# Attention block: the last block's normalisation on VectorE in another order (spread, product, spread, product by column halves)

## The chip, the cores and the metric

One core of a Trainium2 chip. The metric is the device time of one execution in microseconds (us), the median of several runs. The profile's span (first to last instruction) is some 1.8 us shorter than the device time of the same execution: 410.1 against 411.93 for the profiled run of the kernel before. Ends and differences below are taken from the traces' nanoseconds: sums of the rounded figures that the lines show can be off by 0.01 us, also in the prediction.

## The reference, cut to what matters

```python
B, S, D, H = 1, 2048, 448, 16          # bf16; head width 28
qkv = x @ wqkv
scores = jnp.einsum("bhqd,bhkd->bhqk", q, k) * (Dh ** -0.5)
p = softmax(scores)
o = jnp.einsum("bhqk,bhkd->bhqd", p, v)
return o.transpose(...).reshape(B, S, D) @ wo
```

The kernel leaves the softmax's division to the end: it sums exp(scores) along with the products with v, and divides o by that sum before the projection with wo.

## The kernel before: the parts that count

A schedule of some 400 us computes four groups of four heads for four blocks of 512 queries. ScalarE computes 425 exponentials of 128x1024. What follows is the end, for the last group and the last 512 queries. `PO` holds, in PSUM, four heads of 32 rows each, and row 28 of each 32 is the sum. The transpose by 32x32 blocks (128x512, 0.72 us) brings the sums into columns, the reciprocal is taken of 16 columns (0.25 us), and a second transpose, of a broadcast, spreads each reciprocal over the 32 rows of its head (0.45 and 0.40 us for its two halves).

```python
    def norm_dve(src, dt, dr, den):
        nc.vector.transpose(out=dt, in_=src)                      # DT, 512 columns
        nc.vector.reciprocal(out=dr, in_=dt[:, Dh::HP])           # DR, 16 columns
        n = QW // HP // 2
        for hf in range(2):                                       # "spread" 0 and 1
            nc.vector.transpose(out=den(hf), in_=dr[:, hf * n:(hf + 1) * n]
                ...to_broadcast([P, n, HP]))
    # ... (cut: the schedule)
    norm_dve(PO[:], DT[:], DR[:], lambda hf: DEN[hf][:])
    for hf in range(2):                                           # "product" 0 and 1
        nc.vector.tensor_tensor(out=OTL[hf][:], in0=PO[:, hf * hw:(hf + 1) * hw], in1=DEN[hf][:], op=ALU.mult)
        for tq in (2 * hf, 2 * hf + 1):                           # blocks 0,1 and 2,3 of 128 queries
            nc.tensor.matmul(out=fb[tq], lhsT=OTL[hf][:, (tq % 2) * P:(tq % 2 + 1) * P], rhs=WO[:, g, :], ...)
    for tq in range(TPC):
        if tq in SPLIT[c]:                                        # block 2
            nc.vector.tensor_tensor(out=OUTF[tq][:], in0=fb[tq], in1=part(c, tq), op=ALU.add)
        else:                                                     # blocks 0, 1, 3
            nc.scalar.copy(out=OUTF[tq][:], in_=fb[tq])
        (nc.scalar if tq == TPC - 1 else nc.sync).dma_start(out=out_last[:, tq, :], in_=OUTF[tq][:])
```

## Time and profile before

| | kernel before |
|---|---|
| device time, median of 3 runs | 412.26 us (411.98 to 412.35) |
| span of the profiled run | 410.1 us |
| ScalarE's exponentials | 390.8 us in 425 instructions, back to back |
| first exponential starts | 11.20 us |
| transpose of the sums (DT) starts | 402.90 us |
| last store's issue ends | 407.33 us |

The time splits into three stretches: up to the first exponential, the long row of exponentials, and the tail from DT on. The prediction shows the tail's lines with neighbours of one form merged. Narrow slices of the timeline give VectorE's four instructions one by one (start, length, both in us):

```profile
403.94 0.45 DVE L824 STREAM_TRANSPOSE DEN<-DR 128x256 f32<-128x256 f32 x1
404.31 0.40 DVE L824 STREAM_TRANSPOSE DEN<-DR 128x256 f32<-128x256 f32 x1
404.63 0.38 DVE L1243 TENSOR_TENSOR OTL<-PO,DEN 128x256 bf16<-128x256 f32 x1
404.94 0.41 DVE L1243 TENSOR_TENSOR OTL<-PO,DEN 128x256 bf16<-128x256 f32 x1
```

Each of the last three starts 0.07 to 0.08 us before its forerunner ends. None of the three needs what its direct forerunner wrote: product 0 needs spread 0, which lies two back.

### The profile page before, as it was taken

How to read it: one execution, taken by the hardware profiler on the slowest of the kernel's cores; microseconds unless marked ns; L12 is line 12 of the kernel's file. 1: busy time of each engine (PE TensorE's matmuls, PEld its weight loads, DVE VectorE, ACT ScalarE, POOL GpSimd, SP SyncE). 2: the span in 40 equal slices, each digit the busy share in tenths (PEclk: the TensorE clock that was granted, in tenths of full speed). 3: DMA queues.
4: the chain of work that ended last, by engine and by line, in shares of the span. 5: the costliest groups of instructions: out<-in, count | busy, mean ns of one | idle time of the engine just before them, and what ended most of it. 6: DMA issues, size and time to landing. Idle time of an engine off the chain costs nothing.

```text
span 410.1 us, 7564 instructions
## 1 busy us (share of the span) xinstructions
PE 362.4 (88%) x2613; PEld 120.9 (29%) x2613; DVE 395.4 (96%) x701; ACT 397.6 (97%) x437; POOL 225.6 (55%) x217
## 2 busy tenths in 40 slices
PE   8998989898998989899897988989898898989795
PEld 5333232222232232323222232232222222222222
DVE  6999999999999999999999999999999999999995
ACT  4999999999999999999999999999999999999993
POOL 3046557464656656465555646556464655747560
PEclk9999999999999999999999999999999999999999
DMA  9441021012301002111300000000410000001012
GB/s 206 67 74 30 2 57 32 15 53 49 78 2 39 8 28 30 20 38 29 81 18 26 22 15 24 12 26 21 88 38 7 30 12 26 22 27 47 2 71 90
DMA packets 36213, 16.03 MB, mean 39 GB/s; under 512 B 28816, under 2 KB 33296, under 8 KB 36176
## 3 DMA queue, kind: packets, MB, share of 16 engines
q1 hardware_dynamic: 35568, 15.35, 16.2%
q8 instruction: 20, 0.33, 0.3%
q10 hardware_dynamic: 608, 0.22, 0.2%
q14 instruction: 17, 0.14, 0.1%
HBM read 6.91 MB, written 1.96 MB: 22 GB/s over the span
## 4 chain that ended last, share of the span: by engine, by line
ACT 83%; PE 8%; issue 7%; DVE 1%; ACTq 0%
ACT PTA L1121 83%; PE PA L808 3%; PE PO L977 1%; PE PA L355 1%; PE PO L677 0%; ACT RRB L860 0%; PE PD L476 0%; PE PD L376 0%; PE PD L606 0%; PE PD L808 0%; ACT OUTF L1250 0%; PE PO L606 0%; PE PO L476 0%; PE PD L758 0%; DVE DEN L824 0%
## 5 line engine op out<-in xcount | busy, mean ns | idle before, releaser
L1121 ACT ACTIVATE PTA<-PA 128x1024 bf16<-128x1024 f32 x425 | 390.8, 1245 | 0.1
L925 POOL TENSOR_TENSOR DG<-DV,DU 128x512 f16<-128x512 f16 x174 | 200.7, 1155 | 166.1 <-DVE DV L922 156.8
L808 PE MATMUL PA<-QB,KB 64*128 64x512 bf16 x850 | 167.0, 379 | 40.3 <-ACT PTA L1121 38.1
L808 PEld LDWEIGHTS <-KB 64*128 64x128 bf16 x1024 | 66.9, 92 | 185.8 <-issue 177.4
L919 DVE TENSOR_SCALAR DU<-PD 128x512 f16<-128x512 uint16 x174 | 117.4, 679 | 2.7 <-PE PD L808 2.3
L922 DVE SCALAR_TENSOR_TENSOR DV<-PD,DU 128x512 f16<-128x512 uint16 x174 | 117.9, 681 | 1.3
L938 DVE SCALAR_TENSOR_TENSOR PTD<-PD,DG 128x512 uint16<-128x512 f32 x174 | 117.8, 677 | 0.2 <-POOL DG L925 0.2
L977 PE MATMUL PO<-PTA,VA 128*32 128x512 bf16 x850 | 84.9, 386 | 0.0
L808 PE MATMUL PD<-QB,KB 64*128 64x512 bf16 x174 | 64.7, 376 | 1.1 <-DVE PTD L938 0.6
L977 PE MATMUL PO<-PTD,VA 128*32 128x512 bf16 x174 | 60.0, 386 | 0.0
L977 PEld LDWEIGHTS <-VA 128*32 128x32 bf16 x1024 | 18.8, 94 | 45.8 <-issue 45.3
L900 POOL TENSOR_TENSOR OT<-OSB,RRB 128x512 bf16<-128x512 f32 x15 | 19.1, 1270 | 5.4 <-DVE PTD L938 1.9
L606 PE MATMUL PO<-XT,WQP 112*128 112x512 bf16 x56 | 18.5, 386 | 0.0
L476 PE MATMUL PO<-XT,WKP 112*128 112x512 bf16 x52 | 16.4, 385 | 0.1
L677 PEld LDWEIGHTS <-XT 112*128 112x128 bf16 x256 | 13.4, 98 | 10.4 <-issue 10.2
L677 PE MATMUL PO<-WV,XT 112*128 112x112 bf16 x208 | 16.0, 214 | 0.0
L1082 PE MATMUL PO<-zrow,zeros 128*128 128x512 bf16 x45 | 15.4, 386 | 0.0
L616 DVE TENSOR_SCALAR QB<-PO,offscol 128x512 bf16<-128x512 f32 x14 | 10.4, 743 | 1.0 <-PE PO L606 0.8
L511 DVE TENSOR_SCALAR KB<-PO,onescol 128x512 bf16<-128x512 f32 x12 | 8.9, 740 | 0.0
L885 DVE COPY OSB<-PO 128x512 f32<-128x512 f32 x13 | 8.9, 683 | 0.0
L758 PE MATMUL PO<-WO,OT 128*128 128x448 bf16 x28 | 8.2, 358 | 0.0
L515 DVE TENSOR_REDUCE KPART<-KB 128x1 f32<-128x512 bf16 x12 | 7.9, 661 | 0.0
(97 smaller groups left out, 120.6 us busy)
## 6 DMA issues: line engine op xcount, KB each, us to landing
RRB<-SCR SPq DMA_DIRECT2D x15, 256.0 KB
QB<-QP SPq DMA_DIRECT2D x56, 32.0 KB
KB<-NK SPq DMA_DIRECT2D x12, 128.0 KB
XS<-in_x_dram SPq DMA_DIRECT2D x3, 448.0 KB
out_dram<-XS SPq DMA_DIRECT2D x3, 448.0 KB
QB<-QB SPq DMA_DIRECT2D x28, 32.0 KB
KB<-KB SPq DMA_DIRECT2D x6, 128.0 KB
WV<-in_wqkv_dram SPq DMA_DIRECT2D x1, 392.0 KB
```

The costliest lines, as they stand in the source:

```text
L476: ops = chain_mm(CC, lambda cc: nc.tensor.matmul(out=ap(), lhsT=WKP[g][:, cc, :], rhs=XT[sc][cc // 2][0:CK, cc % 2, :], start=(cc == 0), s ...
L606: ops = chain_mm(CC, lambda cc: nc.tensor.matmul(out=ap(), lhsT=WQP[g][:, cc, :], rhs=XT[c][cc // 2][0:CK, cc % 2, :], start=(cc == 0), st ...
L677: nc.tensor.matmul(out=ap()[:, jj * GW:(jj + 1) * GW], lhsT=XT[jq][cc // 2][0:CK, cc % 2, jj * P:(jj + 1) * P], rhs=WV[:, cc, g * GW:(g + ...
L808: nc.tensor.matmul(out=ap, lhsT=KB[g % 2][i // 2][a:a + 64, j * P:(j + 1) * P], rhs=QB[w % NQB][i // 2][a:a + 64, :], start=True, stop=Tru ...
L900: o5 = add(Op("POOL", 1.22, lambda: nc.gpsimd.tensor_tensor(out=OT[g][c][:], in0=OSB[b][:], in1=RRB[b][:], op=ALU.mult), deps=o4, prio=-10 ...
L919: p1 = add(Op("DVE", P1, lambda: nc.vector.tensor_scalar(out=DU[b][:], in0=lo, scalar1=SIG / 65536, scalar2=SIG * (SS - 0.5), op0=ALU.mult ...
L922: p2 = add(Op("DVE", P1, lambda: nc.vector.scalar_tensor_tensor(out=DV[b][:], in0=lo, scalar=65536 * (SS - 0.5 + CE / C3), in1=DU[b][:], o ...
L925: gq = add(Op("POOL", PTT, lambda: nc.gpsimd.tensor_tensor(out=DG[b][:], in0=DV[b][:], in1=DU[b][:], op=ALU.mult), deps=[p2], prio=n, kind ...
L938: f = add(Op("DVE", P1, lambda: nc.vector.scalar_tensor_tensor(out=PTD[st["s"].idx][:].bitcast(U16), in0=PX[slot.idx][:], scalar=EBITS + C ...
L977: nc.tensor.matmul(out=PO[HP * st:HP * (st + 1), :], lhsT=VA[g][:, j, st, :], rhs=r["p"][i][1](), start=first, stop=last, tile_position=(0 ...
L1082: nc.tensor.matmul(out=PO[:], lhsT=zeros[:], rhs=zrow[:], start=first, stop=first, skip_group_check=True)
L1121: nc.scalar.activation(out=PTA[pslot.idx][:, 0:len(ns) * QW], in_=PA[s.idx][:, 0:len(ns) * QW], func=ACT.Exp, bias=ACT_BIAS, scale=ACT_SCALE)
```

## The change

The intent: TensorE's first projection needs product 0, product 0 needs spread 0 alone, so take spread 1 out of its way.

```diff
-    def norm_dve(src, dt, dr, den):
+    def norm_dve(src, dt, dr, den, then):
 ...
         for hf in range(2):
             nc.vector.transpose(out=den(hf), ...)
+            then(hf)
 ...
-    norm_dve(PO[:], DT[:], DR[:], lambda hf: DEN[hf][:])
-    for hf in range(2):
+
+    def half_out(hf):
         nc.vector.tensor_tensor(out=OTL[hf][:], ...)
         for tq in (2 * hf, 2 * hf + 1):
             nc.tensor.matmul(out=fb[tq], ...)
+    norm_dve(PO[:], DT[:], DR[:], lambda hf: DEN[hf][:], half_out)
```

No instruction is added or removed, and TensorE's order stays.

## The prediction

> **What bounds the kernel now.** I read the page's busy row first, then the chain that ended last as a whole, then that chain for the last ten microseconds, then the timeline and the short windows of the tail. The page says who is busy, and by whom the end is set:
>
> ```profile
> PE 362.4 (88%) x2613; PEld 120.9 (29%) x2613; DVE 395.4 (96%) x701; ACT 397.6 (97%) x437; POOL 225.6 (55%) x217
> ACT 83%; PE 8%; issue 7%; DVE 1%; ACTq 0%
> ```
>
> ScalarE (ACT) is busy 97% of the 410.1 us span and carries 83% of the chain: its 425 exponentials (390.8 us) set the pace. VectorE (DVE) is at 96%, but carries only 1% of the chain. The change touches neither loop. It reorders four VectorE instructions that run once, after the last exponential (which ends at 402.32 us). So the steady state stays, and the question is how much of the tail depends on these four. The chain in the tail (start, length, what):
>
> ```profile
> 402.90 0.73 DVE DT L820
> 403.63 0.02 issue
> 403.65 0.27 DVE DR L821
> 403.92 0.02 issue
> 403.94 0.77 DVE DEN L824 x2
> 404.71 0.32 DVE OTL L1243
> 405.03 0.05 issue
> 405.08 0.38 PE PD L1245
> ...
> 405.48 0.59 ACT OUTF L1250 x2
> ```
>
> Here VectorE is the end of the kernel: transpose of the sums (DT), reciprocal (DR), two spreads of the reciprocals (DEN) and two products (OTL). TensorE's first projection waits for the first product, and that product stands behind a second spread it does not need. This is what the change removes. What follows the products is in the timeline:
>
> ```profile
> 404.63 0.72 DVE L1243 TENSOR_TENSOR OTL<-PO,DEN 128x256 bf16<-128x256 f32 x2
> 405.08 0.55 PE L1245 MATMUL PD<-WO,OTL 128*128 128x448 bf16 x2 [0.42 <-DVE OTL L1243]
> 405.46 0.35 PE L1245 MATMUL PA<-WO,OTL 128*128 128x448 bf16 x1
> 405.48 1.40 ACT L1250 CAST OUTF<-PD 128x448 bf16<-128x448 f32 x3 [3.16 <-PE PD L1245]
> 405.65 0.35 PE L1245 MATMUL PD<-WO,OTL 128*128 128x448 bf16 x1
> 405.93 0.62 DVE L1248 TENSOR_TENSOR OUTF<-PA,PARTL 128x448 bf16<-128x448 f32 x1 [0.57 <-PE PA L1245]
> 406.03 1.29 SPq L1251 DMA_DIRECT2D out_dram<-OUTF  x3
> 406.91 0.40 ACTq L1251 DMA_DIRECT2D out_dram<-OUTF  x1
> ```
>
> Four matmuls, one for each 128 query rows (blocks 0 to 3); blocks 0, 1 and 3 are copied by ScalarE, block 2 by VectorE; blocks 0 to 2 are stored through SP, block 3 through ScalarE's queue. ScalarE's three casts are back to back once the first matmul is done: narrow slices of the timeline show them start at 405.48, 405.90 and 406.33. So two things can release the end: the first half of the columns, through that row of casts, or the second half, through matmuls 2 and 3.
>
> [...] Independent neighbours overlap by 0.07 to 0.08 us: spread 0 is 403.94 to 404.39 and spread 1 starts at 404.31. Dependent neighbours do not: DT ends at 403.62 and DR starts at 403.65; DR ends at 403.90 and spread 0 starts at 403.94. So a dependence costs a gap of 0.03 to 0.04 in place of an overlap of 0.08, about 0.11 us for each pair. [...]
>
> **The change part by part.** It removes and adds nothing: two spreads (445 and 401 ns), two products, four matmuls stay, with the same shapes and the same TensorE order. It moves product 0 ahead of spread 1. Three independent neighbours become three dependent or serial steps:
>
> 1. Spread 0 ends at 404.39 as now. Product 0 depends on it: start 404.39 + 0.03 = 404.42, end + 0.38 = 404.80. Before it ended at 404.63 + 0.38 = 405.01. **The first half is 0.21 earlier.**
> 2. Spread 1 does not depend on product 0: overlap 0.07, so 404.73 to 405.13.
> 3. Product 1 depends on spread 1: 405.13 + 0.03 = 405.16, plus 0.41 = 405.57. Before it ended at 404.94 + 0.41 = 405.35. **The second half is 0.22 later.** This is the price: two exposed dependences in place of overlaps, 2 x 0.11.
> 4. TensorE. The last earlier matmul ends at 404.66, so the engine is free. From the end of product 0 to the first matmul is 0.07 (405.01 to 405.08), so matmul 0 starts at 404.87, matmul 1 (0.20 later, as now) at 405.07. Matmul 2 waits for product 1: 405.57 + 0.07 = 405.64 (now 405.46, where it stood right behind matmul 1), matmul 3, 0.19 later, 405.83 (now 405.65).
> 5. ScalarE. From matmul 0's start to the cast is 0.40: casts at 405.27, 405.69, and the third at the later of 405.69 + 0.43 = 406.12 (engine free) and 405.83 + 0.40 = 406.23 (matmul 3). So 406.23 in place of 406.33: only 0.10 of the 0.21 arrives, and the third cast now waits for TensorE. With its 0.55 and 0.03 more, ScalarE issues its store at 406.81 (now 406.91), and ends that at 407.21.
> 6. VectorE's sum of block 2 starts 0.47 after matmul 2: 406.11, ends 0.62 later at 406.73. SP starts at 405.82 and 406.26 for blocks 0 and 1 (0.21 earlier), and its third store at the later of 406.72 (SP starts are 0.44 to 0.46 apart) and 406.73 + 0.03 = 406.76; now 406.93. It ends at 407.15.
> 7. Last issue ends: 407.32 now, 407.21 then: **0.11 less**.
>
> Then the stores have to land. The windows of the tail show the DMA engines busy 0.77, 0.74 and 1.00 of the half microseconds from 407.0 to 408.5, with nothing after 409.0. Four stores of 112 KB therefore partly queue on the DMA engines. If what queues decides, the first store's start counts too, which is 0.21 earlier; if the last issue decides, 0.11. I take 0.14, nearer the last issue: 412.26 - 0.14 = 412.12 us.
>
> **The rivals.** (a) *The first half decides to the end*: all 0.21 arrives. For it: the casts are back to back and the stores queue. Against it: step 5, where matmul 3 comes 0.11 after ScalarE is free. Time 412.05. (b) *The second half takes over fully*: matmul 3 or VectorE's sum is later still, because spread 1 also waits for product 0 [...] (0.11 more), or the dependence gap is longer on these forms. Then product 1 would end at 405.68, the third cast start at 406.34, and the sum end at 406.84: nothing gained or some 0.05 lost, 412.25 to 412.31. For it: both half columns' exposures add to product 1 and nothing else hides there; the margin is as small as the gain. (c) *The change is lost in the DMA tail*: from the last issue's end (407.32) to the last data is some 1.7 us, a time that may wander by more than 0.1. Time 412.26. (d) A shift of the main loop through another placement of the instructions: the instruction stream has the same length and the same order up to 403.94 us, so I see nothing for it.
>
> **The range and the chances.** All rivals lie within 412.05 and 412.31. The three runs of before span 411.98 to 412.35, 0.37 us, more than the whole effect, and the median of a new set can sit anywhere in such a span or a little outside. So 411.75 to 412.55. Two per cent is 8.2 us; the whole piece from the last exponential's end to the end of the span is 7.8 us. Faster or slower by that is out of reach of this edit; I leave 0.01 to each for a chip in another mood.
>
> **What would show each step.** In the changed trace the VectorE tail reads spread, product, spread, product, with product 0 ending some 0.21 earlier against DT's start and product 1 some 0.22 later. Spread 1 overlaps product 0 (else rival b). Matmul 2 has an idle gap before it, released by the product, of about 0.4 us by starts (405.07 to 405.64, less 0.19). The third cast waits for TensorE by about 0.1 us, where it waited for nothing. The last store's issue ends some 4.3 us after DT's start (407.32 - 402.90 = 4.42 now). The prediction is wrong if a dependence costs much more than 0.03, if the stores' landing takes back or adds more than 0.1, or if the body before 402.90 moves at all.

The lengths of the old order (0.38 and 0.41 us in steps 1 and 3) are read from the trace; that they stay the same in another order was the assumption. That the stores partly queue is an estimate from the busy shares of the windows (0.77, 0.74 and 1.00), not shown. TensorE's part is counted from start to start.

## The result, and the profile after

The changed kernel took 411.71 us in the median (411.58 to 411.97, 4 runs). The kernel before had 412.12 (411.94 to 412.35, 4 runs, its first three among them). The ratio is 0.9991, with a 95% interval of 0.9973 to 1.0008. A ratio here is the mean time of one kernel's runs over that of the other's of the same rounds, so not quite the ratio of the medians. The median lies 0.04 us below the predicted range of 411.75 to 412.55, and 0.41 below the predicted 412.12.

VectorE's timeline of the changed kernel's tail:

```profile
403.08 0.72 DVE L820 STREAM_TRANSPOSE DT<-PO 128x512 f32<-128x512 f32 x1 [0.27 <-PE PO L978]
...
404.12 0.45 DVE L824 STREAM_TRANSPOSE DEN<-DR 128x256 f32<-128x256 f32 x1
404.61 0.42 DVE L1244 TENSOR_TENSOR OTL<-PO,DEN 128x256 bf16<-128x256 f32 x1
404.95 0.44 DVE L824 STREAM_TRANSPOSE DEN<-DR 128x256 f32<-128x256 f32 x1
405.42 0.42 DVE L1244 TENSOR_TENSOR OTL<-PO,DEN 128x256 bf16<-128x256 f32 x1
```

DT starts at 403.08 here and at 402.90 before, so the tail must be read from DT's start. Product 0 ends 1.95 us after it (before 2.12), and product 1 2.76 (before 2.45). The first half comes 0.17 us earlier, the second 0.31 later. Each product now starts only after its spread has ended (404.57, then 404.61), and it reads 0.42 us long.

What follows, from the timelines of TensorE and of ScalarE with its store queue:

```profile
405.90 0.36 PE L1246 MATMUL PA<-WO,OTL 128*128 128x448 bf16 x1 [0.26 <-DVE OTL L1244]
406.10 0.35 PE L1246 MATMUL PD<-WO,OTL 128*128 128x448 bf16 x1
405.49 1.53 ACT L1252 CAST OUTF<-PD 128x448 bf16<-128x448 f32 x3 [2.99 <-PE PD L1246]
407.05 0.38 ACTq L1253 DMA_DIRECT2D out_dram<-OUTF  x1
```

The chain of waits (start, length, what) now runs through the second half:

```profile
404.61 0.42 DVE OTL L1244
405.03 0.36 DVE DEN L824
405.39 0.02 issue
405.42 0.44 DVE OTL L1244
405.85 0.05 issue
405.90 0.36 PE PA L1246
406.26 0.20 PE PD L1246
406.47 0.02 issue
406.49 0.53 ACT OUTF L1252
```

Before, it went from product 0 through matmul 0 and the row of casts. Now the third cast waits for matmul 3, which waits for product 1. The store that ends its issue last does so at 407.43 - 403.08 = 4.35 after DT's start, in place of 4.43. And yet this profiled run is not shorter: its span is 410.18 us, that of before 410.13. The tail from DT on is 7.10 against 7.23, but all that lies ahead came 0.18 later. So two questions were left for experiments: what is the tail worth, and where do the other 0.3 us of the medians come from?

### The profile page after: what moved, and what is told of

It is laid out like the page before. It is cut to its first block, busy times and chain, and to the rows that moved or that the text cites. A ratio compares the mean times of both kernels' runs of the same rounds, so it can differ in the third digit from the quotient of the medians.

```text
span 410.2 us, 7553 instructions
## 1 busy us (share of the span) xinstructions
PE 360.2 (88%) x2602; PEld 120.8 (29%) x2613; DVE 395.5 (96%) x701; ACT 397.7 (97%) x437; POOL 225.3 (55%) x217
## 4 chain that ended last, share of the span: by engine, by line
ACT 83%; PE 8%; issue 6%; DVE 1%; ACTq 0%
ACT PTA L1122 82%; PE PA L808 3%; PE PO L978 1%; PE PA L355 1%; PE PO L677 0%; ACT RRB L861 0%; PE PO L606 0%; PE PD L476 0%; DVE XT L387 0%; PE PD L606 0%; PE PD L808 0%; PE PO L476 0%; PE PD L758 0%; PE PD L376 0%; DVE OTL L1244 0%
## 5 line engine op out<-in xcount | busy, mean ns | idle before, releaser
L1083 PE MATMUL PO<-zrow,zeros 128*128 128x512 bf16 x34 | 12.5, 387 | 0.3 <-issue 0.3
L692 DVE CAST VA<-PO 128x448 bf16<-128x448 f32 x13 | 8.0, 617 | 0.0
```

The source lines that it names most:

```text
L1083: nc.tensor.matmul(out=PO[:], lhsT=zeros[:], rhs=zrow[:], start=first, stop=first, skip_group_check=True)
```

## The experiments

Theory A: the tail gained 0.1 to 0.15 us, and the rest of the difference is wander of the stretch ahead of it, whatever the kernel. Theory B: the changed program shifts what lies ahead by some 0.3 us. For the inside of the tail: did the chain really change from the first half to the second, and what does an exposed dependence on VectorE cost?

### The same two kernels again

The first repeats of the kernel before and of the changed kernel: no edit but a comment.

> The kernel before, unchanged, against itself: the noise floor. Theory A (the time that the runs showed beyond the tail's 0.1 us is wander of the body from run to run): the ratio is within 0.9990 to 1.0010, single runs spread by 0.3 us or more, and the transpose of the sums starts somewhere between 402.6 and 403.2 us in the profile. Theory B (the changed code shifts the body itself by some 0.3 us): this kernel stays at its 412.1 us, all runs within 0.4 us.

> The changed kernel, unchanged, once more. Theory A: ratio 0.9995 to 1.0002 (a tail 0.1 us shorter is 0.9997), so within 0.1 us or so of the repeat of the kernel before. Theory B: ratio 0.9985 to 0.9993 again (0.3 to 0.6 us less). In the trace, measured from the start of the transpose of the sums, both theories expect the first product's end at 1.95 us, the second's at 2.76, the last store's issue ending at 4.35.

Measured: the kernel before took 411.71 us (411.68 to 411.95, 5 runs), the changed one 411.82 (411.57 to 412.06, 5 runs), and the runs of the kernel before that both were compared with 411.95 (9 runs). Against these the ratios are 0.9996 (0.9982 to 1.0009) and 0.9998 (0.9985 to 1.0010). The kernel before alone thus gave exactly the changed kernel's first median. Theory B falls. A third pair was run to see where the wander sits:

> The kernel before, unchanged, a third time. If all wander lies ahead of the first exponential: from the first exponential's start to the transpose of the sums 391.70 us within 0.03, and from that transpose to the end of the span 7.22 to 7.29, whatever the total. If the body wanders too: 391.70 does not hold.

> The changed kernel a third time. If the change is worth what its tail shows: 391.70 within 0.03 again, and 7.07 to 7.13 from the transpose to the end (0.14 to 0.17 less than the kernel before). The mean of its timed runs, pooled with the earlier ones, lies 0.05 to 0.25 us below that of the kernel before. If the change shifts the start or the body: first exponential earlier in every run, or not 391.70.

Measured: 411.71 us (411.68 to 411.93) and 411.85 (411.70 to 412.20), five runs each; ratios 0.9999 (0.9987 to 1.0012) and 1.0004 (0.9991 to 1.0016). This time the changed kernel reads slower than the kernel before. The traces say why:

| trace | first exponential | DT's start | between | DT to span's end | span |
|---|---|---|---|---|---|
| before | 11.20 | 402.90 | 391.70 | 7.23 | 410.13 |
| before, second | 11.20 | 402.90 | 391.70 | 7.27 | 410.17 |
| before, third | 10.98 | 402.69 | 391.71 | 7.22 | 409.91 |
| changed | 11.38 | 403.08 | 391.70 | 7.10 | 410.18 |
| changed, second | 10.99 | 402.70 | 391.71 | 7.08 | 409.79 |
| changed, third | 11.62 | 403.31 | 391.69 | 7.09 | 410.40 |

From the first exponential to DT it is 391.69 to 391.71 us in all six. Nearly all the wander lies in the first 11 us, where the exponential starts anywhere from 10.98 to 11.20 (before) or 11.62 (changed). There TensorE waits for x to be loaded (XS). The waits of the first 12 us of the changed kernel, the latest start, third run first and then its second run (us in total, times, longest):

```profile
PEld L376 <- DMA XS<-in_x_dram: 1.7, 3, 1.1
PE PA L376 <- DMA XS<-in_x_dram: 0.6, 1, 0.6
```

```profile
PEld L376 <- DMA XS<-in_x_dram: 0.6, 1, 0.6
```

In the run that started latest, these waits sum to 2.3 us, in the other to 0.6. The sums do not order all the runs (the first run of the kernel before has 1.3 in three waits and starts at 11.20, its repeat 0.5 and starts at 11.20 too), so the load's landing is the likely cause of the wander, not a shown one; that it lies ahead of the first exponential is shown.

### What the tail is worth

By the same table the tail is 7.22 to 7.27 us before and 7.08 to 7.10 after: 0.15 us less by the means (7.24 and 7.09), outside the spread of either. The device times of the same six profiled runs show it too, once each is taken less the start of its first exponential: 400.72 to 400.75 us before, 400.57 to 400.59 after. The totals alone can't resolve this. All timed runs of the kernel before in these studies have a mean of 411.87 us (39 runs), those of the changed kernel 411.84 (14 runs): 0.03 apart, with standard errors of 0.03 and 0.06, where 0.05 to 0.25 was expected. That the starts of the changed kernel's runs happened to be late is likely, but shown only for the profiled ones. The lowest times, presumably the runs that started earliest, are 411.68 and 411.57, 0.11 apart.

### A useless copy: which half decides?

```diff
 # in the kernel before: between its two products
+        if hf == 1:
+            nc.vector.tensor_copy(out=DUM[:], in_=DT[:, 0:QW // 2])
         nc.vector.tensor_tensor(out=OTL[hf][:], ...)
 # in the changed kernel: between product 0 and spread 1
             then(hf)
+            if hf == 0:
+                nc.vector.tensor_copy(out=DUM[:], in_=DT[:, 0:QW // 2])
```

> The kernel before with a VectorE copy of 256 columns that nobody needs between its two products (some 0.2 to 0.3 us). If the first half (the row of three casts) decides in the kernel before, the second half has 0.28 us to spare: matmuls 2 and 3 are later by the copy's start-to-start time, and the last store's issue still ends 4.42 to 4.48 us after the start of the transpose of the sums. Rival (the second half decides already): the issue's end moves by the whole copy, to 4.65 or more.

> The changed kernel with the same useless copy between the first product and the second spread. If the second half decides after the change, the last store's issue ends later by nearly the whole copy: 4.35 + 0.2 to 0.3 = 4.55 to 4.65 us after the start of the transpose of the sums, and the third cast's wait for TensorE grows by the same. Rival (the first half still decides): 4.35 to 4.40.

Measured in the traces, after DT's start (402.67 in both): with the copy (0.27 us long, 0.19 from start to start) the kernel before issues its last store until 4.44, where it was 4.43. Its tail is 7.24, as without the copy. The copy is free there. Its ScalarE casts and its SP store queue (the last issue ends with this row):

```profile
405.25 1.40 ACT L1253 CAST OUTF<-PD 128x448 bf16<-128x448 f32 x3 [3.16 <-PE PD L1248]
405.81 1.30 SPq L1254 DMA_DIRECT2D out_dram<-OUTF  x3
```

Its three casts stay back to back. In the changed kernel the copy (0.28, 0.20 from start to start) moves the last issue's end from 4.34 or 4.35 to 4.54 and the tail from 7.09 to 7.29: all of it arrives. The second and third cast of this kernel and its last issue, from the timeline:

```profile
405.50 0.54 ACT L1255 CAST OUTF<-PD 128x448 bf16<-128x448 f32 x1
406.27 0.53 ACT L1255 CAST OUTF<-PD 128x448 bf16<-128x448 f32 x1 [0.23 <-PE PD L1249]
406.83 0.38 ACTq L1256 DMA_DIRECT2D out_dram<-OUTF  x1
```

ScalarE stands idle for 0.23 us for matmul 3. So the chain did change sides: the first half decides before, the second after. (Both kernels ran once; their totals, 411.69 and 411.74 us, say nothing.)

### Two spreads exchanged: the price of one dependence

```diff
-        for hf in range(2):
+        for hf in (1, 0):
             nc.vector.transpose(out=den(hf), ...)
```

In the kernel before, product 0 now stands right behind the spread that it needs, and nothing else moves.

> The kernel before with only the two spreads exchanged, so that the first product stands right behind the spread that it needs: one dependence exposed, nothing else moved. If an exposed dependence costs the lost overlap of 0.08 us and a gap of 0.03, and the product behind it reads 0.42 us in place of 0.38: the first product starts 0.11 later (1.84 us after the transpose's start) and ends 0.15 later (2.26), the second ends at 2.56 or so, and all that follows is 0.10 to 0.15 later. Rival (the 0.11 belongs to changing between a transpose and a product, not to the dependence): nothing moves, 2.11 and 2.45.

VectorE's timeline (DT starts at 402.68):

```profile
404.08 0.40 DVE L824 STREAM_TRANSPOSE DEN<-DR 128x256 f32<-128x256 f32 x1
404.52 0.42 DVE L1243 TENSOR_TENSOR OTL<-PO,DEN 128x256 bf16<-128x256 f32 x1
404.86 0.41 DVE L1243 TENSOR_TENSOR OTL<-PO,DEN 128x256 bf16<-128x256 f32 x1
```

Product 0 starts at 404.52 - 402.68 = 1.84 us and ends at 2.27, in place of 1.73 and 2.12: 0.11 later by the start, 0.15 by the end. Product 1 ends at 2.60 (some 2.56 was expected). The last issue's end goes to 4.58 (from 4.43), the tail to 7.40 (from 7.24). It is the dependence that costs, not the change between two kinds of instruction, which the kernel before has as well (spread 1, then product 0, with an overlap).

### Forty rounds: the same price by the clock

```diff
     norm_dve(PO[:], DT[:], DR[:], lambda hf: DEN[hf][:])
+    for _ in range(40):
+        spread(0); spread(1); product(0); product(1)      # one kernel
+        spread(0); product(0); spread(1); product(1)      # the other
```

`spread(hf)` and `product(hf)` are the kernel's own two instructions, put into functions. The rounds write the same values again, so the results stay right.

> The kernel before with 40 more rounds of spread, spread, product, product behind its own spreads (they write the same values again). From the trace of before, from start to start, a round takes about 0.37 + 0.32 + 0.31 + 0.33 = 1.33 us, so 53 us more: some 465 us.

> The same with 40 rounds of spread, product, spread, product: from the trace of after 0.49 + 0.34 + 0.47 + 0.34 = 1.64 us for a round, so 66 us more, some 478 us: 12 us more than in the other order, 0.31 us a round, by the clock and not only by the trace. If the exposed dependence were hidden outside what the profiler's records show, both would take the same time, within 1 us.

Measured: 464.63 us (464.50 to 464.77, 4 runs) and 477.04 (476.74 to 477.53, 4 runs), against 411.80 for the kernel before in the same rounds (ratios 1.1281 and 1.1586). A round takes (464.63 - 411.80) / 40 = 1.32 us in the old order and 1.63 in the new: 0.31 us for two exposed dependences (12.4 us more for 80 of them, 0.155 us each). VectorE's groups in that stretch, the old order first, then the new (count, then busy us and mean ns):

```profile
L1246 DVE STREAM_TRANSPOSE DEN<-DR 128x256 f32<-128x256 f32 x80 | 29.9, 411 | 0.0
L1249 DVE TENSOR_TENSOR OTL<-PO,DEN 128x256 bf16<-128x256 f32 x80 | 28.6, 395 | 0.0
```

```profile
L1246 DVE STREAM_TRANSPOSE DEN<-DR 128x256 f32<-128x256 f32 x80 | 34.7, 434 | 0.0
L1249 DVE TENSOR_TENSOR OTL<-PO,DEN 128x256 bf16<-128x256 f32 x80 | 34.0, 425 | 2.8
```

The same instructions read 23 and 30 ns longer in the new order. The price of 0.31 us is thus made of the gaps, the lost overlaps and this length.

### An uneven cut in the old order

If the row of casts decides before, then only block 0 has to come early. This kernel keeps both spreads ahead of both products and cuts the columns into 128 and 384.

```diff
-    DEN = [sb([P, QW // 2], F32, f"DEN{i}") for i in range(2)]
+    CUT = (0, P, QW)
+    DEN = [sb([P, CUT[i + 1] - CUT[i]], F32, f"DEN{i}") for i in range(2)]
 # OTL, the spreads and the products likewise; matmuls:
-        for tq in (2 * hf, 2 * hf + 1):
+        for tq in ((0,), (1, 2, 3))[hf]:
```

> The old order (both spreads, then both products), with the columns cut into 128 and 384 in place of 256 and 256, so only the first block of rows goes early. If the chain of three casts on ScalarE is what decides as long as the second half is not made later: first product ends 0.13 us earlier than before (1.98 us after the transpose's start), second where it was (2.45), casts 0.13 earlier, the last store's issue ends at 4.29 to 4.32 us after the transpose's start (before 4.42, after 4.35), without the price that the changed order pays. Rival (the second half decides in both): issue's end stays at 4.42. Time: 0.1 us less than before, not to be told from noise.

> The 128/384 cut in the old order a second time: tail 7.09 to 7.13 us, like the changed kernel's, first exponential anywhere between 10.97 and 11.4, 391.70 between. The mean of the timed runs 0.05 to 0.25 us below that of the kernel before.

The products, from the timeline of the first run (DT starts at 402.69):

```profile
404.42 0.25 DVE L1244 TENSOR_TENSOR OTL<-PO,DEN 128x128 bf16<-128x128 f32 x1
404.60 0.54 DVE L1244 TENSOR_TENSOR OTL<-PO,DEN 128x384 bf16<-128x384 f32 x1
```

Product 0 ends at 1.99 and product 1 at 2.45, as expected, and the last issue ends at 4.30 in both runs: 0.04 earlier than in the changed kernel, 0.13 earlier than before. (The first cast comes 0.13 us earlier, as expected, the other two only 0.09 to 0.10: the second now waits a little for matmul 1, which stands behind product 1.) But the tail is 7.11 and 7.14 us, no shorter than the changed kernel's 7.09. By the clock: 411.64 (411.59 to 411.98) and 411.67 us (411.59 to 412.02), five runs each, ratios 0.9995 (0.9982 to 1.0008) and 0.9998 (0.9984 to 1.0012). From the first exponential to DT it is 391.70 and 391.71 again. So the old order with another cut gains in the tail nearly what the new order gains (0.12 us by the means, against 0.15), and neither can be told from the kernel before by its time. (The mean of its ten runs is 411.74 us, 0.13 below that of the kernel before, with a standard error of 0.05.)

Why the earlier issue did not bring an earlier end stays open. From the end of the last issue to the end of the span it is 2.79 to 2.84 us where SP's last issue ends 0.02 to 0.03 us after ScalarE's (before, with the copy, with the spreads exchanged, uneven), and 2.74 to 2.76 where ScalarE's ends 0.07 to 0.08 after SP's (changed, also with the copy). In both forty-round kernels ScalarE's ends last too, but by 0.20, and there it is 2.63 us. So the queue alone doesn't set this stretch. Over these three groups (13 traces) it is the longer the closer together the two last issues end, but whether the one causes the other is not shown: no run moves one store alone or exchanges the queues. The DMA packets in the traces say that the difference is mostly in the landing: the last packet ends 1.31 to 1.33 us after the last issue in the first group, 1.27 to 1.29 in the second and 1.16 in the forty-round kernels; from there to the end of the span it is 1.46 to 1.52 in all.

## Why the prediction was right or wrong

**The bound and the stage: right.** The change acted on the tail alone. From the first exponential to DT it took the same 391.70 us in all 13 traces, within 0.02, so rival (d), a shift of the main loop, is out.

**The sign of each half and the change of sides: right; their sizes were off.** Steps 1 and 3 put an exposed dependence at 0.11 us (a gap of 0.03 and a lost overlap of 0.08), so the first half at 0.21 earlier and the second at 0.22 later. Measured: 0.17 earlier and 0.31 later. The gap (0.03) and the lost overlap were right: product 0 starts 0.21 earlier. The term "2 x 0.11" was mis-sized, for I gave product 0, spread 1 and product 1 the lengths that they have in the old order (0.38, 0.40 and 0.41), on the assumption, which no run had shown, that the order of the products does not change their length. In the new order they read 0.42, 0.44 and 0.42, 0.09 us more in sum: product 0 reads longer right behind the spread that it needs (the exchange of the spreads shows the same 0.42), and spread 1 reads 0.44 where it doesn't stand behind another spread (here behind product 0, in the kernel with the useless copy behind that copy; spread 0 reads 0.45 behind the reciprocal). One dependence is 0.15 to 0.16 (0.15 in the exchange of the spreads, 0.31 / 2 in the forty rounds).

**What waits, by the traces.** In the old order each of the last three instructions starts 0.07 to 0.08 us before its forerunner ends, and none needs what that forerunner wrote. In the new order product 0 starts 0.03 us after its spread has ended. That it is the dependent neighbour which waits here is read from these traces, and from the exchange of the spreads above all (the start 0.11 later).

**Steps 4 to 6: right in kind.** Matmul 2 waits for product 1 (it starts 405.90 - 405.29 = 0.61 after matmul 1, which less 0.19 is 0.42; 0.4 was expected). The third cast waits for TensorE: it could start 0.42 after the second (406.34) and started at 406.49, so 0.15 late where 0.1 was expected. **Step 7** expected the last issue to end 0.11 earlier; it was 0.08 (4.43 to 4.35), 0.09 by the means of three traces each.

**The tail's sum: right in size, and not for the reason given.** I took 0.14, between the 0.11 of the last issue and the 0.21 of the first store, on my estimate that the stores queue. The tail shrank by 0.15. But in the changed kernel with the useless copy, the first store is as early as in the changed kernel while the last issue is 0.19 later, and from the last issue to the end it is 2.75 us as in the changed kernel. If the first store's start counted, that stretch should have been shorter. The 0.15 is 0.09 of earlier issue and 0.06 after it, of which 0.04 is quicker landing, whose cause is the open point above, and 0.02 lies behind the last packet. That the sum came out as 0.14 is thus partly luck. (Rival (c) put the last data some 1.7 us after the last issue; in the kernel before the last packet ends after 1.31 to 1.33.) So rivals (b) and (c) are both half true: the second half does take over, but not fully, and for neither reason that (b) gave (spread 1 overlaps product 0 by 0.08, and the gap is 0.03); and the last microseconds do differ, in our favour.

**The range: wrong, and this is the step that failed.** "The three runs of before span 411.98 to 412.35, 0.37 us [...] the median of a new set can sit anywhere in such a span or a little outside. So 411.75 to 412.55." I took the median of these three, 412.26, for the kernel's time and a few tenths around it for its wander. But those three were on the high side of it. The same kernel read 411.95, 411.80, 411.72 and, as its own test kernel, twice 411.71 us; 17 of its 39 runs lie between 411.68 and 411.72, a floor that none of the first three came near. In the traces the wander comes from the first 11 us, where the first exponential starts between 10.97 and 11.62. A sharper sum for the tail would not have helped; 411.87, the mean of all runs of the kernel before, less 0.14 would have been 411.73, beside the measured 411.71. That the measured number fell just outside the range is partly luck too: the changed kernel's later sets have medians of 411.82 and 411.85, inside it. The 0.41 between predicted and measured median is nearly all base, not change.

## What to carry to other kernels

On VectorE's queue, try to put something independent between an instruction and the one that needs its result: with these spreads and products an exposed dependence cost 0.15 to 0.16 us. Spread, spread, product, product was the faster order for the four together (1.32 us a round against 1.63), and taking the stranger out brought the first result 0.17 us earlier at the price of 0.31 for the last. Ask which of the two the end waits for, and how much slack the other has (here at least the 0.19 us that a useless copy could fill at no cost): an early start for a small first piece can be had without the price, as the uneven cut shows (product 0 at 1.99 us in place of 2.12, product 1 still at 2.45). And before a change of a tenth of a microsecond is predicted or judged, split the span at fixed marks in several traces: the stretch that you did not touch may wander more than your change is worth (here 0.22 us over three traces of the kernel before and 0.63 over three of the changed one, for a change of 0.15).
